# Two orders changed in a three-layer kernel: chunk 2's place in a pair, and drains before weight stages

## Chip, cores and metric

The kernel runs on one core of a Trainium2 chip. The metric is the device time of one execution in microseconds (us), taken as the median of several runs. The profile is of one execution of its own.

## What is computed

The reference chains three layers over 1536 tokens of width 512. First comes attention with 8 heads over two sequences of 768, with a window and a few sink positions. Then a two-layer block with 2048 hidden units:

```python
h = x @ w_in
g = np.maximum(h, 0.0) + alpha * np.minimum(h, 0.0)
return (g @ w_out).astype(np.float32)
```

Last come four experts of 1024 hidden units, weighted per token:

```python
for e in range(E):
    h = np.maximum(x @ w1[e], 0.0)
    out += p[:, e:e + 1] * (h @ w2[e])
```

All inputs are 32-bit floats. The kernel splits each matrix operand into a rounded high part and a low part (hi, lo) and adds three products, hi·hi, hi·lo and lo·hi, so a logical matmul is three on TensorE (PE).

## The kernel before, in words

**Tiling.** Tokens are cut into three chunks (c = 0, 1, 2) of 512 columns, or six units of 256. Hidden units are cut into 48 slices of 128 (NW): 16 of the second layer (N1), then 32 of the experts. A slice k has a weight tile pair wh[k], wl[k] that holds both its first-layer and its second-layer weights. `s1` (lines 250 to 252) makes a slice's hidden values h for one chunk with 12 matmuls; `s2_transposed` (259 to 261) and `s2_natural` (268 to 270) add the slice into the output sums in PSUM, again 12 matmuls. Between them stands `prelu` (283 to 286: two operations on VectorE (DVE), one on ScalarE (ACT) for the high part gh, one on GpSimd (POOL) for the low part gl) or `relu` (292 on ACT, 297 on DVE).

**Weight stages.** Raw weights come by DMA from the SP queue into four buffers. `half(j)` (lines 102 to 122) turns half a slice into hi and lo parts in three stages that use ACT (102, 104, 120), DVE (107 to 109, sometimes 122) and POOL (110, sometimes 122). `pair(j)` (135, 136, 143) does so for two expert slices in eight stages, on ACT and POOL alone. `tick()` starts the next generator in a queue and moves every generator in flight by one stage; `ready(k)` ticks until slice k is complete. So where a tick stands in the program sets where the stage's instructions stand in the in-order queues of ACT, DVE and POOL. A load is issued by `load_due` once the buffer's last reader has been written out.

**fast and rest.** `fast` runs the attention, mixed with the second layer's slices 0 to 5 for units 0 to 4, in a loop over p whose last turn is p = NP + 3. `rest` runs the remaining steps in a list: unit 5 with slices 0 to 5 (256 columns), then three blocks of slices (6 to 10, 11 to 15, and the first two of the experts, 16 and 17) for each of the three chunks. In turn i it writes out `s1` and `prelu` or `relu` of step i and `s2` of step i - 2, then one tick, and, at the last slice of a block, four drains of the PSUM sums into the accumulators acc (lines 859, 862 or 871 on DVE; at block 2 also lines 864 and 865, the split of the new x). `sums` (313 to 326) makes combinations of the accumulators that the experts need, seven pieces in all, one per turn.

**Experts.** From slice 18 (PAIR1) on, slices go in pairs, 15 of them. For the first layer of chunks 0 and 1 together `four(k)` (lines 354 to 366) computes seven block products, 42 matmuls, in place of eight. Its last two low parts, of c21 and c12, are put into `self.later` as functions that `leave` runs. `out(k, c, hid)` (395 to 400) is the second layer of a pair for one chunk: four output tiles d of six matmuls each, every one followed by one DVE operation that adds the weighted result to acc (line 400). Its PSUM tiles alternate between two buffers, so tile d + 2 waits for the acc of tile d. `out` runs one waiting function of `later` after each acc, and ticks after d = 1 and d = 3. Chunk 2 has a plain first layer: `s1` for both slices.

In `experts` a turn is: four(k); out of chunk 2 of the pair before, whose hidden values were kept in `last`; s1 and relu of chunk 2 for this pair; one tick; what is left in `later`; out of chunks 0 and 1. After the last turn chunk 2's out of the last pair follows, and at that pair each acc is followed by its output DMA.

Of the kernel before, what the change touches and what calls it, by code (L numbers as in the profile page):

```python
# [28 lines left out]
N1 = F1 // P  # L29
NW = N1 + E * (F2 // P)  # L30
# [15 lines left out]
STARTS = [1, 3, 5, 9, 10, 12, 13, 14, 16, 18, 20, 22, 46, 48, 49, 50]  # L46
# [7 lines left out]
class Body:  # L54
# [70 lines left out]
    def pair(self, j):  # L125
# [16 lines left out]
        def minus(out, a, b):  # L142
            nc.gpsimd.tensor_tensor(out, a, b, ALU.subtract)
# [191 lines left out]
    def four(self, k):  # L335
# [26 lines left out]
        def add(out, a, b):  # L362
            nc.vector.tensor_tensor(out, a, b, ALU.add)  # L363
# [23 lines left out]
    def out(self, k, c, hid):  # L387

        nc, mm, e = self.nc, self.nc.tensor.matmul, (k - N1) * P // F2
        for d in range(CH // P):  # L390
            ps = self.psum[1].tile([P, CH], F32, tag="o", name=f"o{k}_{c}_{d}", bufs=2)
            n = slice(d * P, (d + 1) * P)
            for x, (hh, hl) in enumerate(hid):
                wh, wl = self.wh[k + x][:, CH:], self.wl[k + x][:, CH:]
                mm(ps, hh[:, n], wh, start=x == 0, stop=False)  # L395
                mm(ps, hh[:, n], wl, start=False, stop=False)  # L396
                mm(ps, hl[:, n], wh, start=False, stop=x == 1)  # L397
            nt = c * (CH // P) + d
            acc = self.acc[c][:, d, :]
            nc.vector.scalar_tensor_tensor(acc, ps, self.prob[:, nt, e:e + 1], acc, ALU.mult, ALU.add)  # L400
            self.leave(1)
            if d % 2:
                self.load_due()
                self.tick()
            if k == NW - 2:
                nc.sync.dma_start(self.a["out"][nt * P:(nt + 1) * P, :], acc)

    def leave(self, n=None):
        for step in self.later[:n]:
            step()  # L410
        del self.later[:n]

    def experts(self):
        last = None
        for k in range(PAIR1, NW, 2):
            if k > PAIR1:
                self.four(k)
            if last:
                self.out(k - 2, 2, last)
            if k + 4 < NW:  # L420
                self.queue.append(2 * (k + 4))
            last = []
            for x in range(2):
                ps = self.psum[0].tile([P, CH], F32, tag="o", name=f"h{k}_c{x}", bufs=2)
                self.s1(k + x, self.xh[2], self.xl[2], ps)
                last.append(self.relu(ps, f"{k}_c{x}"))
            self.load_due()
            self.tick()
            self.leave()
            for c in range(2):  # L430
                self.out(k, c, self.hid[k][c])
        self.out(NW - 2, 2, last)


    def positions(self):
# [251 lines left out]
    def fast(self):  # L687
# [5 lines left out]
        with tc.tile_pool(name="psa", bufs=1, space=PSUM) as self.psa:  # L693
# [10 lines left out]
            NP, items, before = NU * H, [], None  # L704
# [10 lines left out]
            for p in range(NP + 4):  # L715
                if p + 1 >= WHOLE:
                    self.at_load(p + QK + 1)
                self.at_split(p + 2)
                for j in [0, 1] if p == 0 else [p + 1] if p + 1 < SOON else [] if p < SOON else [p]:
                    self.at_scores(j)  # L720
                    if j == 0:
                        self.busy(psb, BETWEEN, "busy", tag="h", bufs=2)
                    if j < WHOLE:
                        self.at_load(j + QK)
                if p > max(LOADS) or p in LOADS:
                    self.load_due(1)
                if FILL.get(p):
                    self.busy(psb, FILL[p], f"busy{p}", tag="h", bufs=2)
                self.at_mask(p)
                if p == 1:  # L730
                    next(self.later_masks)
                if p % 2:
                    self.at_sinks(p - 3)
                self.at_exp(p)
                if p % 2 == 0:
                    self.at_values(p - 4)
                    self.at_scale(p - 4)
                    self.at_norm(p - 2)
                self.at_split_lo(p + 2)
                if p == 2 * H:  # L740
                    self.shares()
                turn = [p - 1]
                while items and items[0][0] < p + 1:
                    _, what, step = items.pop(0)
                    u, f, first, last = step
                    n = slice(u % 2 * UN, (u % 2 + 1) * UN)
                    if what == "s1":
                        ps = psb.tile([P, CH], F32, tag="h", name=f"h{u}_{f}", bufs=2)
                        self.ready(f)
                        self.s1(f, self.xh[u // 2][:, :, n], self.xl[u // 2][:, :, n], ps[:, :UN])  # L750
                        while turn:
                            self.at_turn(turn.pop())
                        gs[step] = self.prelu(tmp, ps[:, :UN], UN, f, f"a{u}_{f}")
                        continue
                    if first:
                        outs = [psb.tile([P, 2, UN], F32, tag="o", name=f"o{u}_{f}_{i}", bufs=2) for i in range(2)]
                    self.s2_transposed(
                        f, *gs.pop(step), [outs[d // 2][:, d % 2, :] for d in range(4)], first, last, [True, False] * 2
                    )
                    while turn:  # L760
                        self.at_turn(turn.pop())
                    if last:
                        for i in range(2):
                            acc = self.acc[u // 2][:, 2 * i:2 * i + 2, n]
                            if u in seen:
                                nc.vector.tensor_tensor(acc, outs[i], acc, ALU.add)
                            else:
                                nc.vector.tensor_copy(acc, outs[i])
                        seen.add(u)
                while turn:  # L770
                    self.at_turn(turn.pop())
                if p % 2 == 0:
                    self.at_x(p - 4)
                if p == NP + 3:
                    tmp.release()
                    at.release()
                    self.add_late()
                self.tick(p in STARTS)
                if p == NP - 1:
                    self.atk.release()  # L780
                    self.add_late()
                    self.plan(*range(EARLY, SLOTS))
# [12 lines left out]
    def rest(self, pool, units, blk0):  # L795

        nc, tc = self.nc, self.tc
        n1 = len(BLOCKS) - 1
# [4 lines left out]
        last = {s[3]: i for i, s in enumerate(steps)}  # L803
# [5 lines left out]
        sums = self.sums()  # L809
        with tc.tile_pool(name="psc", bufs=1, space=PSUM) as psc:  # L810
            psum = self.psum = [self.psb, psc]
            gs, outs = {}, None
            for i in range(len(steps) + 2):
                if i < len(steps):
                    k, c, n, f = steps[i]
# [10 lines left out]
                self.leave()  # L826
                i -= 2
                if i < 0:
                    continue
                k, c, n, f = steps[i]  # L830
                nn = n.stop - n.start
                f0, f1 = BLOCKS[k][0], BLOCKS[k][0] + BLOCKS[k][1] - 1
# [13 lines left out]
                while PAIR1 <= nxt < PAIR1 + 4 and last[nxt + 1 - SLOTS] <= i:  # L846
                    self.queue.append(2 * nxt)
                    nxt += 2
                self.tick()
                if (k, c) in [(n1 - 1, 2), (n1, 0), (n1, 1)] and (c, f) != (1, N1 + 1):  # L850
                    next(sums, None)
                if f < f1:
                    continue
                if k == n1 - 1:
                    self.new_x(c, "y")
                for d in range(4):
                    acc = self.acc[c][:, d, n]
                    if k == 0:
                        nc.vector.tensor_copy(acc, outs[d])
                        continue  # L860
                    if k < n1:
                        nc.vector.tensor_tensor(acc, outs[d], acc, ALU.add)
                        if k == n1 - 1:
                            nc.scalar.activation(self.xh[c][:, d, :], acc, AF.Copy)
                            nc.gpsimd.tensor_tensor(
                                self.xl[c][:, d, :], acc, self.xh[c][:, d, :].bitcast(F32), ALU.subtract
                            )
                        continue
                    nt = c * (CH // P) + d
                    pr = self.prob[:, nt, k - n1:k - n1 + 1]  # L870
                    nc.vector.tensor_scalar(acc, outs[d], pr, None, ALU.mult)
            self.experts()


# [147 lines left out]
```

## Time and profile before

| what | us |
|---|---|
| median of 3 runs | 923.92 |
| lowest and highest run | 923.84, 926.82 |
| the profiled execution's own time | 927.69 |
| its span from the first to the last instruction | 925.5 |

Times in the profile count from the span's start. In that execution `rest` begins on PE at about 212 us, the first pair of experts at 431 us, and the second pair at 463 us. A pair from the second on takes 32.3 us. PE, DVE, ACT and POOL each work through their queue in order; a bracket behind a row gives the idle time of the engine before the instruction and what ended it.

### The profile page before, as it was taken

How to read it: one execution, taken by the hardware profiler on the slowest of the kernel's cores; microseconds unless marked ns; L12 is line 12 of the kernel's file. 1: busy time of each engine (PE TensorE's matmuls, PEld its weight loads, DVE VectorE, ACT ScalarE, POOL GpSimd, SP SyncE). 2: the span in 40 equal slices, each digit the busy share in tenths (PEclk: the TensorE clock that was granted, in tenths of full speed). 3: DMA queues.
4: the chain of work that ended last, by engine and by line, in shares of the span. 5: the costliest groups of instructions: out<-in, count | busy, mean ns of one | idle time of the engine just before them, and what ended most of it. 6: DMA issues, size and time to landing. Idle time of an engine off the chain costs nothing.

```text
span 925.5 us, 12401 instructions
## 1 busy us (share of the span) xinstructions
PE 903.0 (98%) x4670; PEld 742.2 (80%) x4670; DVE 549.3 (59%) x999; ACT 316.2 (34%) x719; POOL 371.6 (40%) x346
## 2 busy tenths in 40 slices
PE   8999999998999999999999999999999999999997
PEld 5678999998878888887878777877887787778786
DVE  6578877647994553546555455455545545554554
ACT  4587767754331222332222121222212122221210
POOL 2366654535673454674414332341433234143100
PEclk9699999999999999999999999999999999999999
DMA  6554442201331010011011101110110101010003
GB/s 187 153 166 146 157 127 91 76 1 69 134 118 46 23 68 1 1 35 35 23 47 35 46 11 46 35 37 20 35 46 12 46 34 42 16 37 9 1 1 141
DMA packets 23718, 54.47 MB, mean 59 GB/s; under 512 B 3168, under 2 KB 3168, under 8 KB 23648
## 3 DMA queue, kind: packets, MB, share of 16 engines
q1 hardware_dynamic: 23504, 53.57, 17.6%
q8 instruction: 39, 0.64, 0.3%
q14 instruction: 31, 0.25, 0.1%
q10 hardware_dynamic: 144, 0.00, 0.0%
HBM read 50.42 MB, written 3.15 MB: 58 GB/s over the span
## 4 chain that ended last, share of the span: by engine, by line
PE 85%; DVE 12%; issue 1%; ACT 1%; POOL 0%; DVEq 0%; ACTq 0%; POOLq 0%
PE o L395 8%; PE o L397 8%; PE o L396 8%; PE h L354 5%; PE h L356 5%; PE h L355 5%; PE h L250 4%; PE h L251 4%; PE h L252 4%; PE o L259 4%; PE o L260 4%; PE o L261 4%; PE pv L646 3%; PE h_c L250 3%; PE h_c L251 3%; PE h_c L252 3%
## 5 line engine op out<-in xcount | busy, mean ns | idle before, releaser
L136 POOL TENSOR_TENSOR wl<-wraw,wh 128x512 fp32r<-128x512 f32 x60 | 78.3, 1306 | 294.0 <-ACT wh L135 294.0
L400 DVE SCALAR_TENSOR_TENSOR acc<-o,prob,acc 128x512 f32<-128x512 f32 x180 | 134.8, 749 | 77.4 <-PE o L397 76.5
L395 PE MATMUL o<-wh,hh 128*128 128x512 f32 x240 | 93.4, 389 | 0.0
L396 PE MATMUL o<-wl,hh 128*128 128x512 f32 x240 | 93.4, 389 | 0.0
L397 PE MATMUL o<-wh,hl 128*128 128x512 f32 x240 | 93.4, 389 | 0.0
L250 PE MATMUL h<-xh,wh 128*128 128x256 f32 (+1 forms) x264 | 90.4, 342 | 0.0
L252 PE MATMUL h<-xh,wl 128*128 128x256 f32 (+1 forms) x264 | 87.9, 333 | 0.0
L251 PE MATMUL h<-xl,wh 128*128 128x256 f32 (+1 forms) x264 | 87.8, 332 | 0.0
L286 POOL TENSOR_TENSOR gl<-qk,gh 128x512 fp32r<-128x512 f32 (+1 forms) x36 | 49.2, 1369 | 77.8 <-ACT gh L285 75.5
L285 ACT ACTIVATE gh<-qk 128x512 fp32r<-128x512 f32 (+1 forms) x36 | 21.5, 598 | 123.4 <-DVE qk L284 123.4
L297 DVE SCALAR_TENSOR_TENSOR hl_c<-h_c,hh_c 128x512 fp32r<-128x512 f32 x30 | 20.8, 693 | 71.1 <-ACT hh_c L292 71.1
L292 ACT ACTIVATE hh_c<-h_c 128x512 fp32r<-128x512 f32 x30 | 18.0, 599 | 131.7 <-PE h_c L252 131.7
L363 DVE TENSOR_TENSOR wraw<-h,wraw 128x512 f32<-128x512 f32 x45 | 31.1, 692 | 51.0 <-PE h L356 49.4
L283 DVE TENSOR_SCALAR qk<-h,alpha 128x512 f32<-128x512 f32 (+1 forms) x36 | 25.3, 703 | 57.3 <-PE h L252 56.7
L259 PE MATMUL o<-gh,wh 128*128 128x512 f32 (+1 forms) x144 | 54.4, 378 | 4.3 <-ACT gh L285 2.5
L366 ACT ACTIVATE wraw<-h 128x512 f32<-128x512 f32 x15 | 9.0, 599 | 137.9 <-PE h L356 137.9
L250 PEld LDWEIGHTS h<-xh,wh 128*128 128x128 f32 x264 | 50.1, 190 | 6.6 <-issue 1.7
L260 PE MATMUL o<-gl,wh 128*128 128x512 f32 (+1 forms) x144 | 54.5, 378 | 0.5 <-POOL gl L286 0.5
L395 PE MATMUL o<-wh,hh_c 128*128 128x512 f32 x120 | 48.3, 402 | 6.2 <-DVE acc L400 6.2
L261 PE MATMUL o<-gh,wl 128*128 128x512 f32 (+1 forms) x144 | 54.3, 377 | 0.0
L252 PEld LDWEIGHTS h<-xh,wl 128*128 128x128 f32 x264 | 50.0, 189 | 5.3 <-DVE wl L122 0.3
L251 PEld LDWEIGHTS h<-xl,wh 128*128 128x128 f32 x264 | 50.1, 190 | 4.9
(172 smaller groups left out, 2388.8 us busy)
## 6 DMA issues: line engine op xcount, KB each, us to landing
wraw<-in_w SPq DMA_DIRECT2D x32, 512.0 KB, 3.6
wraw<-in_w SPq DMA_DIRECT2D x64, 256.0 KB, 2.6
qk<-in_qk SPq DMA_DIRECT2D x21, 352.0 KB, 2.9
v<-in_v SPq DMA_DIRECT2D x12, 256.0 KB, 3.2
out<-acc SPq DMA_DIRECT2D x12, 256.0 KB, 2.2
qk<-in_qk SPq DMA_DIRECT2D x8, 272.0 KB, 3.3
qk<-in_qk SPq DMA_DIRECT2D x11, 176.0 KB, 3.1
qk<-in_qk SPq DMA_DIRECT2D x8, 136.0 KB, 3.5
```

Source lines behind the costliest of these rows:

```text
L136: nc.gpsimd.tensor_tensor(lo, x, hi.bitcast(F32), ALU.subtract)
L250: mm(ps, wh[:, c], xh[:, dk, :], start=dk == 0, stop=False)
L251: mm(ps, wh[:, c], xl[:, dk, :], start=False, stop=False)
L252: mm(ps, wl[:, c], xh[:, dk, :], start=False, stop=dk == DM // P - 1)
L259: mm(outs[dt], wh[:, c], gh, start=first and begins[dt], stop=False, skip_group_check=True)
L260: mm(outs[dt], wh[:, c], gl, start=False, stop=False, skip_group_check=True)
L261: mm(outs[dt], wl[:, c], gh, start=False, stop=last, skip_group_check=True)
L286: nc.gpsimd.tensor_tensor(gl, g, gh.bitcast(F32), ALU.subtract)
L395: mm(ps, hh[:, n], wh, start=x == 0, stop=False)
L396: mm(ps, hh[:, n], wl, start=False, stop=False)
L397: mm(ps, hl[:, n], wh, start=False, stop=x == 1)
L400: nc.vector.scalar_tensor_tensor(acc, ps, self.prob[:, nt, e:e + 1], acc, ALU.mult, ALU.add)
```

## The change

There are two parts.

**In the experts**, chunk 2's s1 stands directly behind four(k), and chunk 2's out of the same pair stands behind the outs of chunks 0 and 1. The waiting low parts of c21 and c12 are written out behind the first of the two s1 calls, ahead of chunk 2's own relu; `out` no longer runs them.

**In rest**, the drains of a block's sums stand ahead of the tick and of the piece of `sums`. The tick in the last turn of `fast` is dropped, and two ticks are added in the first two turns of `rest`, behind the prelu of steps 0 and 1. The list of turns that run `sums` is shortened to the seven that do something.

```diff
             nc.vector.scalar_tensor_tensor(acc, ps, self.prob[:, nt, e:e + 1], acc, ALU.mult, ALU.add)
-            self.leave(1)
             if d % 2:
...
-    def leave(self, n=None):
-        for step in self.later[:n]:
-            step()
-        del self.later[:n]
+    def leave(self):
+        while self.later:
+            self.later.pop(0)()
 
     def experts(self):
-        last = None
         for k in range(PAIR1, NW, 2):
             if k > PAIR1:
                 self.four(k)
-            if last:
-                self.out(k - 2, 2, last)
             if k + 4 < NW:
                 self.queue.append(2 * (k + 4))
             last = []
             for x in range(2):
                 ps = self.psum[0].tile([P, CH], F32, tag="o", name=f"h{k}_c{x}", bufs=2)
                 self.s1(k + x, self.xh[2], self.xl[2], ps)
+                self.leave()
                 last.append(self.relu(ps, f"{k}_c{x}"))
             self.load_due()
             self.tick()
-            self.leave()
-            for c in range(2):
-                self.out(k, c, self.hid[k][c])
-        self.out(NW - 2, 2, last)
+            for c, hid in enumerate(self.hid[k] + [last]):
+                self.out(k, c, hid)
...
-                self.tick(p in STARTS)
+                if p < NP + 3:
+                    self.tick(p in STARTS)
...
                 if i < 0:
+                    if units:
+                        self.tick()
                     continue
...
-                self.tick()
-                if (k, c) in [(n1 - 1, 2), (n1, 0), (n1, 1)] and (c, f) != (1, N1 + 1):
-                    next(sums, None)
-                if f < f1:
-                    continue
-                if k == n1 - 1:
+                if f == f1 and k == n1 - 1:
                     self.new_x(c, "y")
-                for d in range(4):
+                for d in range(4 if f == f1 else 0):
...
+                self.tick()
+                if (k, c) in [(n1 - 1, 2), (n1, 0)]:
+                    next(sums)
```

## Rows read from the trace of the kernel before

**Rows 1.** The page's part 1: busy us (share of the span), instructions, per engine.

```profile
PE 903.0 (98%) x4670; PEld 742.2 (80%) x4670; DVE 549.3 (59%) x999; ACT 316.2 (34%) x719; POOL 371.6 (40%) x346
```

**Rows 2.** Waits of PE: who waited for whom, total us, times, longest.

```profile
PE o L395 <- DVE acc L400: 6.2, 13, 0.5
PE o L259 <- ACT gh L285: 2.5, 1, 2.5
...
PE o L259 <- DVE acc L862: 1.8, 1, 1.8
...
PE o L268 <- DVE acc L871: 1.1, 1, 1.1
```

**Rows 3.** Timeline, third pair: start, us, engine, line, operation, [idle before].

```profile
505.08 0.39 PE L395 MATMUL o<-wh,hh_c 128*128 128x512 f32 x1
...
507.24 1.30 POOL L136 TENSOR_TENSOR wl<-wraw,wh 128x512 fp32r<-128x512 f32 x1 [12.10 <-ACT wh L135]
...
507.31 1.77 DVE L297 SCALAR_TENSOR_TENSOR hl<-qk,hh 128x512 fp32r<-128x512 f32 x1
...
509.01 0.74 DVE L400 SCALAR_TENSOR_TENSOR acc<-o,prob,acc 128x512 f32<-128x512 f32 x1
...
509.80 0.50 PE L395 MATMUL o<-wh,hh_c 128*128 128x512 f32 x1 [0.48 <-DVE acc L400]
...
511.31 0.39 PE L250 MATMUL h_c<-yh,wh 128*128 128x512 f32 x1
```

**Rows 4.** Timeline of DVE in the last pair.

```profile
895.05 0.68 DVE L297 SCALAR_TENSOR_TENSOR hl<-qk,hh 128x512 fp32r<-128x512 f32 x1
```

**Rows 5.** Timeline of PE in the last pair, the places of rows 3.

```profile
892.82 0.39 PE L395 MATMUL o<-wh,hh_c 128*128 128x512 f32 x1
...
898.26 0.39 PE L250 MATMUL h_c<-yh,wh 128*128 128x512 f32 x1
```

**Rows 6.** Timeline of POOL, one pair: first and last of eight.

```profile
550.55 1.30 POOL L136 TENSOR_TENSOR wl<-wraw,wh 128x512 fp32r<-128x512 f32 x1 [8.01 <-ACT wh L135]
...
557.22 1.30 POOL L136 TENSOR_TENSOR wl<-wraw,wh 128x512 fp32r<-128x512 f32 x1
```

**Rows 7.** Line 400: all 180 acc operations, ns min/median/max.

```profile
L400 DVE SCALAR_TENSOR_TENSOR acc<-o,prob,acc x180: 736/751/752, 453.7 to 920.2; 128x512 f32<-128x512 f32 x180
```

**Rows 8.** Timeline of PE where rest begins, steps 2, 0 and 1.

```profile
212.79 0.28 PE L250 MATMUL h<-xh,wh 128*128 128x256 f32 x1
...
216.99 0.28 PE L252 MATMUL h<-xh,wl 128*128 128x256 f32 x1
219.73 0.38 PE L259 MATMUL o<-gh,wh 128*128 128x256 f32 x1 [2.46 <-ACT gh L285]
220.59 0.58 PE L260 MATMUL o<-gl,wh 128*128 128x256 f32 x1 [0.48 <-POOL gl L286]
...
224.80 0.28 PE L259 MATMUL o<-gh,wh 128*128 128x256 f32 x1
```

**Rows 9.** Windows: length, busy us by engine, PE's granted clock, DMA.

```profile
220.00:224.00 4.00, 3.52 (x18) 3.41 (x18) 1.22 (x3) 2.51 (x5) 1.96 (x3) 0.57 0.31 100
```

**Rows 10.** Timeline of DVE, same place: end of fast, first prelu.

```profile
214.16 1.28 DVE L768 COPY acc<-o 128x512 f32<-128x512 f32 x2
...
218.17 0.48 DVE L283 TENSOR_SCALAR qk<-h,alpha 128x256 f32<-128x256 f32 x1
```

**Rows 11.** Timeline of DVE at the drain of slices 6 to 10, chunk 0.

```profile
270.54 1.65 DVE L109 SCALAR_TENSOR_TENSOR wraw<-cm,wraw 128x512 int32<-128x512 int32 x1
272.12 2.47 DVE L862 TENSOR_TENSOR acc<-o,acc 128x512 f32<-128x512 f32 x4
```

**Rows 12.** Timeline of DVE at sums, ahead of line 871's drain.

```profile
418.54 3.40 DVE L314 TENSOR_TENSOR yl<-wraw,yh 128x512 fp32r<-128x512 f32 x2 [0.87 <-ACT yh L313]
```

**Rows 13.** Waits of PE's weight loads (PEld), columns as in rows 2.

```profile
PEld h L252 <- DVE wl L122: 0.3, 1, 0.3
```

**Rows 14.** DMA issues, raw weights: count, KB each, us to landing.

```profile
wraw<-in_w SPq DMA_DIRECT2D x32, 512.0 KB, 3.6
```

## Prediction

> **What bounds the kernel now.** I read the page first. TensorE is busy 98% of the span, the next engine 59% [rows 1]; so time can come only from PE's own idle stretches, and the question is how many of these the two new orders close. The second view is therefore the list of PE's waits [rows 2]. One row stands out by its count: 13 times a second-layer matmul of line 395 waits for an accumulator operation of line 400. The other three come once each, all in the part called rest: a gh, and two drains of a block's sums.
>
> The third view is the timeline around one of the 13. In chunk 2's out the accumulator operation of tile d = 1 starts at 509.01, because DVE first ran a waiting low part (line 297) of 1.77 us, and PE's next tile starts only at 509.80 after an idle 0.48 [rows 3]. That low part took so long beside POOL, which began a weight piece at 507.24 [rows 3]; in the last pair, where no weights are left, the same operation takes 0.68 [rows 4] and nothing waits. What a wait costs is more than its idle figure, since PE also restarts slowly: chunk 2's out lasts from 505.08 to 511.31, 6.23 us [rows 3], against 892.82 to 898.26, 5.44 us, in the last pair [rows 5]. So one wait of 0.48 costs 0.79, that is 0.31 beyond its idle time.
>
> **The change, part by part.** No matmul, no DVE operation and no DMA is added or removed: the same instructions come in another order. *Experts.* The stall needs two things at once: low parts in DVE's queue between accumulator operations, and PSUM tiles that alternate between two buffers. The change takes the first away. Behind four(k) PE now runs chunk 2's s1, 24 matmuls, 5.4 us at the rate of the last pair [rows 5], and these wait for no DVE result of four(k). In that time DVE does the last addition of four (taken at 0.74, as the accumulator operation [rows 3]) and the two low parts: with 0.68 for each of these [rows 4] 2.1 us, and with 1.77 for each [rows 3] 4.3 us. Both fit under 5.4, so out of chunk 0, which needs c12's low part, finds it ready. Gain: 13 x 0.79 = 10.3 us.
>
> What is late next there? Every moved instruction has to be placed. The last two weight pieces of a pair (ticks in chunk 2's out) move from behind four(k + 2) to ahead of it. POOL then does its burst of eight, 550.55 to 558.52 [rows 6], and these two, some 3 us, in one run of 11 us, behind chunk 2's second relu. Three outs last 3 x 5.44 = 16.3 us [rows 5], so POOL is done before four begins, and DVE's waiting low parts meet no POOL. The burst does lie beside accumulator operations, but it did so before, and all 180 took 736 to 752 ns [rows 7]. ACT's pieces go in front of its first copy in four; they finish with POOL's burst. The SP queue's raw loads follow the pieces that free the buffers, so none is later against its use. The last pair's outs and the output DMAs keep their place at the end: nothing there.
>
> *Start of rest.* PE finishes the s1 of steps 0 to 2 at 216.99, waits until 219.73 for gh and until 220.59 for gl, and starts step 1's s2 at 224.80 [rows 8]. The wait also lowered the granted clock: 0.57 over 220 to 224 [rows 9], that is mostly the 1.2 GHz level instead of 2.4, behind 2.7 us without a matmul. Before it, 35 starts of matmuls of 256 columns took from 212.79 to 216.99 [rows 8], 0.12 us each, so the 25 starts from 216.99 to 224.80 need 3.0 of these 7.8 us: 4.8 us lost. The cause is DVE's order: the sums are copied by 215.44, but prelu starts at 218.17 [rows 10], because the stages of fast's last tick stand between. The change puts these 2.7 us of stages behind prelu of step 0. Prelu then starts at 215.44. From prelu's start to the second matmul took 220.59 - 218.17 = 2.42 us, so that matmul comes at 217.86, where a PE without waits would have it at 217.23: 0.63 still lost. Step 1's prelu comes behind 0.95 of prelu and 2.7 of stages, at 219.1, its second matmul at 221.5, wanted at 217.86 + 24 x 0.12 = 220.7: 0.8 still lost. Gain 4.8 - 1.4 = 3.4 us. Gaps so short should not lower the clock: in the pairs a wait of 0.48 costs 0.79 in all [rows 3, 5]. Upper end 4.8; lower end 1.4, if steps 1 and 2 each lose 1 us more because a single stage operation of line 109 takes 1.65, as at 270.54 [rows 11], where all the stages between copy and prelu took 2.7 here.
>
> On this term a rule bears: the Trainium skill, "SBUF — State Buffer", section "Who interferes with whom", says that a DVE instruction with two SBUF inputs is held by a GpSimd instruction that reads SBUF for all of that instruction's time, and a DVE instruction with one SBUF input is not. The slow row of line 297 and the steady rows of line 400 agree. The rule speaks against the new order here, since stages with two SBUF inputs now run beside POOL's gl; by it the lower end, and a sum of 15.2, would be right.
>
> *Drains in front.* PE waits 1.8 us for a drain that DVE reaches only at 272.12, behind a stage operation of 1.65 us that began at 270.54 and others before it [rows 2, 11]. The drain needs only matmuls that PE ended before a whole s1 (2.7 us), so at the head of the queue it is done in time: gain 1.8 + 0.3 = 2.1. The drain near 421.9 stands behind two pieces of sums of 3.40 us [rows 12]; moved ahead, it gains 1.1 + 0.3 = 1.4 [rows 2]. The stages and pieces now wait for 2.5 us of drain instead; their results are needed one turn (24 matmuls, 5.4 us) later or more. Bounds for these two: 2.5 (one of them half kept) to 3.9, with the small waits on drains elsewhere.
>
> **Sum.** 10.3 + 3.4 + 2.1 + 1.4 = 17.2 us. The profiled execution took 927.69, its span 925.5; so such an execution would take 910.5. It lies 3.8 above the median of 923.92; I take the gain as the same there: **906.7**. Bounds of the terms: 9.5 (one pair keeps its wait) to 10.3, 1.4 to 4.8, 2.5 to 3.9; with them 904.9 to 910.5.
>
> **Rivals.** (a) *The weights take it back.* The slices of the first block come just in time now: a weight load of line 252 once waits 0.3 us for a low part that DVE makes in line 122 [rows 13]. A PE that arrives 3.4 us earlier would wait there for as long, and the 2.1 of the drain behind it may go the same way. Against it: the two added ticks start the stages of slices 7 to 10 one turn earlier, and following the queue by hand, only one forced tick of ready(k) is left there instead of two. Time: 923.9 - 10.3 - 1.4 = 912.2.
>
> (b) *The 13 waits move instead of going.* If chunk 0's out found c12's low part late, or POOL's run reached into four, the 0.79 would be paid elsewhere in each pair. Against it is the slack of 1.1 to 3.3 us worked out above. Time: 923.9 - 6.9 = 917.0.
>
> (c) *Slower: ACT is held by a raw load.* A stage begins with an ACT operation on a raw buffer. Started one turn earlier, it may stand at the head of ACT's queue while the load, 3.6 us to landing [rows 14], is still under way, with the next gh behind it and PE behind that. It is only the place from step 0 to slice 13, 12 halves; it decides once more than 17.2 / 3.6, about five, of them hold PE for the whole landing. With all twelve it gives 906.7 + 43 = 950. Against it: loads are issued as early against the stages as before, two turns ahead.
>
> (d) *Nothing moves:* the 13 waits have another cause that the order leaves alone: 923.9. The undisturbed last pair speaks against it.
>
> **How the numbers follow.** Forecast 0.78, (a) 0.10, (b) 0.06, (c) 0.03, (d) 0.03. The range reaches from 903.5, a little under the forecast's own lower bound, for what runs differ, to 912.5, which takes in (a): together 0.88, less some for sizes outside the bounds. About 0.3% (2.8 us) is what a measurement of this kernel can tell from no change. The forecast, (a) and (b) are faster, (d) is the same, (c) slower: 0.94, 0.03, 0.03.
>
> **What would show it.** Right: the row of 13 waits of line 395 is gone, chunk 2's out takes 5.4 us in every pair, a pair from four to four 31.5 instead of 32.3, the low parts of line 297 from qk all take near 0.7, and line 400 stays at 0.75. At the start of rest no gap of PE over 1 us and a clock of 1.00 over 220 to 224; no wait for line 862, or for line 871 ahead of line 268. Wrong: a new wait of PE in s1 of slice 10 (a), on line 297 ahead of line 395 (b), or ACT waiting on raw weights between 215 and 280 (c).

## The result, and the profile after

| us | before | after |
|---|---|---|
| median | 923.88 (4 runs, 922.47 to 926.82) | 911.19 (4 runs, 906.78 to 911.72) |
| profiled execution, its span | 927.69, 925.5 | 906.78, 905.0 |

The ratio is 0.985, 95% interval 0.9817 to 0.9884, so the kernel is faster by 1.5%, clear of no change. The time lies within the range that was given (903.5 to 912.5), 4.5 us above its point of 906.7 and 0.7 above 910.5, up to which the bounds of the forecast's own terms reached. One program does not always take the same time here: how long PE's granted clock stays low near 22 us differs between executions, and since the profiled execution of after has a short fall and that of before a long one, the two spans may not simply be subtracted.

PE is still what bounds the kernel; DVE, which lost 19 us of busy time against [rows 1], ran no operation less. The page of after, part 1:

```profile
PE 891.7 (99%) x4670; PEld 739.1 (82%) x4670; DVE 530.0 (59%) x999; ACT 317.2 (35%) x719; POOL 365.0 (40%) x346
```

The waits of PE in after (who waits for whom, total us, times, longest):

```profile
PE o L260 <- POOL gl L286: 1.9, 3, 0.8
...
PE o L259 <- ACT gh L285: 0.5, 1, 0.5
```

All four rows of [rows 2] have gone or shrunk: the 13 waits and both drains are not there, the 2.5 for gh is 0.5. One wait has grown: before, PE waited once for the low part gl of line 286, for 0.48 [rows 8]; now it does so three times, for 1.9 in all.

Where the time went is seen by cutting the span at four of PE's matmuls: the first s1 of `rest`, the first s1 of 512 columns behind unit 5, the first matmul of the first `four`, and the last matmul of all. The first column below is the time of the first of these starts in the timeline, the next three are the times from each to the next, and behind the span stands the mean granted clock over 20 to 40 us.

| us | rest begins | unit 5 | blocks, to the first four | experts | span | clock |
|---|---|---|---|---|---|---|
| before | 212.79 | 19.21 | 199.04 | 488.76 | 925.5 | 0.57 |
| after | 207.84 | 17.86 | 195.20 | 478.31 | 905.0 | 0.91 |
| change | (−4.95) | −1.35 | −3.84 | −10.45 | | |
| experts_only | 212.19 | 19.18 | 198.73 | 478.29 | 914.2 | 0.57 |
| rest_only | 212.53 | 17.86 | 195.20 | 488.63 | 919.9 | 0.57 |
| drains_only | 207.79 | 20.36 | 196.24 | 488.59 | 918.7 | 0.91 |
| quiet_out2 | 207.80 | 19.15 | 198.72 | 478.27 | 909.9 | 0.91 |
| after_again | 207.86 | 17.72 | 195.20 | 478.31 | 905.0 | 0.91 |
| no_first_ticks | 207.84 | 14.99 | 197.73 | 478.28 | 904.9 | 0.91 |
| second_tick_only | 212.63 | 16.03 | 195.82 | 478.29 | 908.5 | 0.57 |
| more_fill | 207.31 | 17.84 | 195.20 | 478.27 | 904.4 | 1.00 |
| before_fill | 208.09 | 20.47 | 198.72 | 488.65 | 921.7 | 1.00 |
| fill_second_tick | 207.43 | 16.03 | 195.20 | 478.28 | 902.9 | 1.00 |
| leave_late | 207.91 | 17.84 | 195.20 | 553.81 | 980.7 | 1.00 |

In this pair of profiles the change is worth 1.35 + 3.84 + 10.45 = 15.6 us; the 4.95 ahead of `rest` is not its doing. Kernels without any edit of that stage show 212.2 to 212.8 with a clock of 0.57 in one execution and 207.8 with 0.91 in another: experts_only and quiet_out2 run the same program up to there. Two of the three terms depend on the pair that is taken. The five kernels that start `rest` as before does take 19.15 to 20.47 for unit 5, and the three others with the blocks as before take 198.72 or 198.73 for them, not 199.04. Between before_fill and more_fill the sum is 2.63 + 3.52 + 10.38 = 16.5 us.

In the experts the timeline of PE in the third pair of after shows chunk 2's out from 515.92 to the next four at 521.36:

```profile
515.92 0.39 PE L395 MATMUL o<-wh,hh_c 128*128 128x512 f32 x1
...
521.36 0.39 PE L354 MATMUL h<-yh,wh 128*128 128x512 f32 x1
```

That is 5.44 us instead of the 6.23 of [rows 3]. All low parts of line 297, and all acc operations of line 400, in after (ns, least/median/most):

```profile
L297 DVE SCALAR_TENSOR_TENSOR hl<-qk,hh x30: 680/687/694, 431.5 to 879.3; 128x512 fp32r<-128x512 f32 x30
...
L400 DVE SCALAR_TENSOR_TENSOR acc<-o,prob,acc x180: 750/751/752, 443.6 to 899.6; 128x512 f32<-128x512 f32 x180
```

No low part takes the 1.77 of [rows 3] any more, and line 400 stays where [rows 7] had it.

At the start of `rest` four short waits are left. PE in after:

```profile
212.77 0.39 PE L260 MATMUL o<-gl,wh 128*128 128x256 f32 x1 [0.34 <-POOL gl L286]
...
216.29 0.39 PE L259 MATMUL o<-gh,wh 128*128 128x256 f32 x1 [0.51 <-ACT gh L285]
...
217.49 0.39 PE L260 MATMUL o<-gl,wh 128*128 128x256 f32 x1 [0.81 <-POOL gl L286]
...
224.28 0.39 PE L260 MATMUL o<-gl,wh 128*128 128x256 f32 x1 [0.79 <-POOL gl L286]
```

They come at steps 0, 1 (two) and 3, together 2.45 us of idle time. The clock does not fall there: the windows of after (length, busy us of PE, PEld, DVE, ACT, POOL, granted clock, DMA share, GB/s) have 1.00 where [rows 9] had 0.57:

```profile
216.00:220.00 4.00, 2.89 (x22) 2.69 (x23) 2.77 (x5) 1.93 (x5) 3.20 (x3) 1.00 0.57 207
220.00:224.00 4.00, 3.50 (x30) 3.29 (x28) 2.90 (x6) 1.99 (x4) 0.99 (x2) 1.00 0.44 160
```

The reason for the waits is in DVE's queue. The weights of the second layer arrive as 64-bit floats (not every input has 32 bits, as was said at the start): half a slice, 128x512 values, is 512 KB [rows 14]. Lines 102 to 110 make a 32-bit float of the two words of each value; these are the stages that share DVE and POOL with prelu here. The timeline of DVE in after, from the prelu of step 0 (210.40) past those of steps 1 (214.86) and 3 (221.65):

```profile
210.40 0.48 DVE L283 TENSOR_SCALAR qk<-h,alpha 128x256 f32<-128x256 f32 x1
...
212.00 1.27 DVE L109 SCALAR_TENSOR_TENSOR wraw<-cm,wraw 128x512 int32<-128x512 int32 x1
213.63 1.31 DVE L122 TENSOR_TENSOR wl<-wraw,wh 128x512 fp32r<-128x512 f32 x1 [0.36 <-ACT wh L120]
214.86 0.47 DVE L283 TENSOR_SCALAR qk<-h,alpha 128x256 f32<-128x256 f32 x1
...
221.04 0.69 DVE L122 TENSOR_TENSOR wl<-wraw,wh 128x512 fp32r<-128x512 f32 x1 [2.19 <-ACT wh L120]
221.65 0.48 DVE L283 TENSOR_SCALAR qk<-h,alpha 128x256 f32<-128x256 f32 x1
```

and POOL over the first part of it:

```profile
211.99 0.73 POOL L286 TENSOR_TENSOR gl<-qk,gh 128x256 fp32r<-128x256 f32 x1 [0.31 <-ACT gh L285]
213.35 1.04 POOL L110 TENSOR_TENSOR wraw<-wraw 128x512 int32<-128x512 int32 x1 [0.63 <-DVE wraw L109]
```

Two stage operations that take 0.69 where POOL is quiet (as at 221.04) take 1.27 and 1.31 beside these two, each of which had started first. So the prelu of step 1 starts 4.46 us behind that of step 0, and the prelu of step 3 stands behind a stage for which DVE waits 2.19 us on ACT.

The drains now start DVE's work of their turn. DVE in after, at the two places of [rows 11, 12]:

```profile
260.69 2.47 DVE L854 TENSOR_TENSOR acc<-o,acc 128x512 f32<-128x512 f32 x4
263.08 1.28 DVE L107 TENSOR_SCALAR wraw<-wraw 128x512 int32<-128x512 uint32 x1
...
408.80 2.72 DVE L863 TENSOR_SCALAR acc<-o,prob 128x512 f32<-128x512 f32 x4
411.43 2.38 DVE L314 TENSOR_TENSOR yl<-wraw,yh 128x512 fp32r<-128x512 f32 x2
```

### The profile page after: what moved, and what is told of

Read it like the earlier page. It is cut to its first block, busy times and chain, and to the rows that moved or that the text cites. A ratio compares the mean times of both kernels' runs of the same rounds, so it can differ in the third digit from the quotient of the medians.

```text
span 905.0 us, 12418 instructions
## 1 busy us (share of the span) xinstructions
PE 891.7 (99%) x4670; PEld 739.1 (82%) x4670; DVE 530.0 (59%) x999; ACT 317.2 (35%) x719; POOL 365.0 (40%) x346
## 4 chain that ended last, share of the span: by engine, by line
PE 92%; DVE 4%; ACT 1%; issue 1%; POOL 0%; DVEq 0%; ACTq 0%; POOLq 0%
PE o L397 9%; PE o L396 9%; PE o L395 9%; PE h L354 5%; PE h L356 5%; PE h L355 5%; PE h L250 5%; PE h L251 5%; PE h L252 5%; PE o L259 5%; PE o L260 5%; PE o L261 4%; PE h_c L250 3%; PE pv L640 3%; PE h_c L251 3%; PE h_c L252 3%
## 5 line engine op out<-in xcount | busy, mean ns | idle before, releaser
L572 ACT ACTIVATE p<-p,nmax 128x288 f32<-128x288 f32 (+1 forms) x96 | 47.8, 500 | 15.9 <-DVE nmax L551 15.8
L396 PEld LDWEIGHTS o<-wl,hh 128*128 128x128 f32 x240 | 45.0, 188 | 9.4
L395 PEld LDWEIGHTS o<-wh,hh 128*128 128x128 f32 x240 | 45.0, 188 | 9.4
```

## The experiments

Line numbers shift by a few from kernel to kernel; the stages of the table above are meant throughout. Where nothing else is said, the ratio is to the kernel before in the same set of runs.

**The two halves of the change.** experts_only is the first part of the diff alone:

```diff
-            if last:
-                self.out(k - 2, 2, last)
...
+                self.leave()
                 last.append(self.relu(ps, f"{k}_c{x}"))
...
+            for c, hid in enumerate(self.hid[k] + [last]):
+                self.out(k, c, hid)
```

> The changed order of the experts with rest as before. Theory (the two parts are independent, 13 waits at 0.79 us each): the 13 waits of line 395 for line 400 go, the pairs become 31.5 us long, the waits at the start of rest and on the two drains stay as in rows 2; 10.3 us less than before. Rival (the parts lean on each other: part of the gain in the pairs came from rest reaching them in another state): some of the 13 waits stay, gain under 8 us.

Measured 916.33 (912.92 to 918.06, 6 runs), ratio 0.9895 [0.986, 0.9929]. PE's waits:

```profile
PE o L259 <- ACT gh L285: 2.5, 1, 2.5
...
PE o L259 <- DVE acc L856: 1.8, 1, 1.8
...
PE o L268 <- DVE acc L865: 1.1, 1, 1.1
```

As expected, the 13 are gone, the three of `rest` are all there, and the experts take the 478.3 of after. rest_only is the second part alone:

```diff
-                self.tick(p in STARTS)
+                if p < NP + 3:
+                    self.tick(p in STARTS)
...
+                    if units:
+                        self.tick()
...
+                self.tick()
+                if (k, c) in [(n1 - 1, 2), (n1, 0)]:
+                    next(sums)
             self.experts()
```

> The changed order of rest with the experts as before. Theory: the 13 waits stay at 0.48 each; the experts start 5.2 us earlier after the start of rest than before (1.3 us at unit 5's steps, 3.9 us at the drains); 5 us less than before. Rival (the earlier arrival is given back in the experts): under 2.8 us less.

Measured 921.26 (915.48 to 922.09, 12 runs), ratio 0.994 [0.9916, 0.9964]. PE's waits:

```profile
PE o L395 <- DVE acc L400: 6.2, 13, 0.5
PE o L260 <- POOL gl L286: 1.9, 3, 0.8
```

Here the 13 stay and the three waits for gl appear. Stage by stage the halves add up to the change, with no interplay: −10.45 in the experts from one, −1.35 and −3.84 from the other.

**The drains without the ticks.** drains_only is the kernel before with the drains ahead of tick and sums, and with the last tick of `fast` left where it was:

```diff
-                self.tick()
...
-                if k == n1 - 1:
+                if f == f1 and k == n1 - 1:
                     self.new_x(c, "y")
-                for d in range(4):
+                for d in range(4 if f == f1 else 0):
...
+                self.tick()
```

> Only the drains ahead of the tick and of sums; the ticks at the start of rest and the experts as before. Theory: the waits on line 862 and on line 871 ahead of line 268 go, the wait of 2.5 us for gh at the start stays with its stretch at half clock; 3.5 to 3.9 us less than before. Rival (the drains are in time only because the two early ticks moved the weight stages ahead): a wait for a weight part or a drain near slice 10 of 1 us or more remains; 1.4 to 2.5 us less.

Measured 919.97 (917.93 to 924.76, 12 runs), ratio 0.9961 [0.9934, 0.9987]. The blocks take 196.24, that is 2.8 less than in before and 2.5 less than in the other kernels with the old blocks, under the 3.5 to 3.9 of the theory and over what its rival left. Waits of PE:

```profile
PE o L259 <- ACT gh L285: 2.5, 1, 2.5
...
PE h L252 <- POOL wl L122: 0.3, 1, 0.3
```

Both waits on drains are gone, and the wait for gh stays as expected. New is an s1, of slice 9, that waits for its weights. So the drains in front give most of the blocks' gain, but about 1 us of it (196.24 against 195.20) is kept only if the stages start earlier, as the two added ticks make them.

**Is it POOL beside the low parts?** quiet_out2 leaves the old order of the experts and takes only the weight pieces away from chunk 2's out: its two ticks go behind the out of chunk 1.

```diff
-            if d % 2:
+            if d % 2 and c < 2:
                 self.load_due()
                 self.tick()
...
             for c in range(2):
                 self.out(k, c, self.hid[k][c])
+            for _ in range(2):
+                self.load_due()
+                self.tick()
```

> The order of before in the experts and in rest, but the two ticks inside chunk 2's out are moved behind chunk 1's out, so that POOL has no weight piece while DVE runs the two waiting low parts. Theory (the wait comes from low parts that POOL stretches to 1.77 and 1.10 us): every low part from qk takes 0.68 to 0.70, the 13 waits go without the new place of chunk 2's first layer, and the time falls by 10.3 us, as with the new order. Rival (two more DVE operations in the queue between the accumulations are enough, with or without POOL): the 13 waits stay, shorter or not, and the time falls by under 3 us.

Measured 910.67 (909.03 to 917.18, 6 runs), ratio 0.9859 [0.9817, 0.9902]. The low parts, between the same acc operations as before:

```profile
L297 DVE SCALAR_TENSOR_TENSOR hl<-qk,hh x30: 679/682/693, 436.2 to 880.6; 128x512 fp32r<-128x512 f32 x30
```

The experts take 478.27, as with the new order. The ticks carry copies on ACT as well, but in after 15 of the 30 low parts ran beside an operation of ACT and took 0.68. So the cause of the 13 waits was not the low parts' place by itself but the place beside POOL's weight pieces. Either cure does: move the low parts, or move the pieces.

**The same kernel again.** after_again is the changed kernel without an edit, to see how its executions spread.

> The changed kernel once more, to have its runs beside the others on one chip. Both theories: executions fall into groups by the granted clock of the core, as before's do (919.3 at 0.999, 922.3 at 0.995, 926.8 at 0.988). Theory (the groups come from the clock in the first 60 us, which the change does not touch): the same groups lie 15 to 16 us lower, some 911.3 at 0.989 and 904 to 907 above. Rival (the new order makes the core's clock fall less): the groups are not parallel, and 0.988 is missing.

Measured 905.2 (904.94 to 906.76, 6 runs), ratio 0.9781 [0.9752, 0.981]. All six have a mean granted clock of 0.998 or 0.999, as the profiled execution has with 0.997; the other three of the four executions behind the 911.19 had 0.989 (911.05 to 911.72). The kernel before shows 919.2 to 919.8 at 0.999, 922.0 to 923.9 at 0.994 or 0.995, and 926.1 to 929.9 at 0.986 to 0.991. Like against like, 926.8 less 911.3 is 15.5, as the theory has it, but at 0.999 the middle of each, 919.5 less 905.1, is 14.4, less than it said.

**The price of the added ticks.** no_first_ticks drops them:

```diff
-                    if units:
-                        self.tick()
                     continue
```

> The changed kernel without the two ticks in the first two turns of rest (the last tick of the attention loop stays dropped). Theory (the waits that are left at the start of rest, 3.3 us, come from the stages of these ticks between the first prelus): the steps of unit 5 take 14.5 to 15.5 us instead of 17.9, but slices 9 and 10 are staged one turn later and PE waits there for 1 to 3 us, as the rival on the weights in the prediction said; within 1.5 us of the changed kernel. Rival (the staging has slack): no wait at slices 9 and 10, 2.5 to 3.3 us faster.

Measured 910.87 (904.8 to 911.97, 6 runs), ratio 0.9831 [0.9796, 0.9867]. Unit 5 falls from 17.86 to 14.99, but the blocks rise from 195.20 to 197.73. Both are as the theory has them. PE's waits and the place of the first:

```profile
PE h L252 <- POOL wl L122: 1.8, 1, 1.8
...
PE o L260 <- POOL gl L286: 0.3, 1, 0.3
...
239.26 0.50 PE L252 MATMUL h<-xh,wl 128*128 128x512 f32 x1 [1.81 <-POOL wl L122]
```

This is rival (a) of the prediction at work, in s1 of slice 9: a PE that arrives 2.9 us earlier meets weights that are not ready, and 2.5 of the 2.9 are paid there. So the two added ticks gain nothing over none: 14.99 + 197.73 = 212.72 us without them, 213.06 with them. They only carry the loss from one place to another. second_tick_only keeps one of the two:

```diff
-                    if units:
+                    if units and i == -1:
                         self.tick()
```

> The changed kernel with a tick in the second turn of rest only. Following the queue by hand, the stages are as far along from turn 3 on as with both ticks. Theory (the place of the stages between the prelus sets what is lost): the waits before step 1's second layer, 1.7 us, go, one of up to 1 us before step 2's or step 3's stays; 1 to 2 us faster than the changed kernel. Rival (the chain from ACT to DVE to POOL is what limits, wherever the ticks stand): the waits only move by a step; within 0.6 us of the changed kernel.

Measured 909.72 (908.85 to 910.41, 6 runs), ratio 0.9827 [0.9798, 0.9855], all six at a mean clock of 0.989 to 0.991. From the start of `rest` to the first four it takes 16.03 + 195.82 = 211.85, against 213.06 in after. PE's waits:

```profile
PE o L260 <- POOL gl L286: 1.1, 2, 0.8
...
PE h L252 <- DVE wl L122: 0.2, 1, 0.2
```

One tick is enough for the weights but for 0.2 us, and costs less at the start. Over this stretch it beats after by 1.2 us, as the theory had it; against the executions of after at 0.989 it is 1.6 us faster.

**The clock ahead of rest.** more_fill is the changed kernel with two more filler matmuls in turn 3 of `fast` and one more in turn 4 (a filler reads no result and keeps PE at work); before_fill is the same edit in the kernel before.

```diff
-WARM, FILL = 6, {p: 1 for p in range(11)}
+WARM, FILL = 6, {p: {3: 3, 4: 2}.get(p, 1) for p in range(11)}
```

> The changed kernel with two more filling matmuls in turn 3 of the attention loop and one more in turn 4, where PE stands idle for 0.6 and 1.0 us at about 20 us and the granted clock then falls for 4 to 15 us. They compute nothing that is used. Theory (these idle stretches let the clock fall): the clock stays at 1.00 over 20 to 40 us in the profile, the group of executions at 0.988 is gone, and the median falls by 4 to 7 us. Rival (the clock falls whatever stands there): the same groups, each 0 to 1.5 us later for the added matmuls.

> The kernel before with the same three added filling matmuls. Theory (the clock's fall at 20 us is one and the same in both kernels and the fill removes it): one group of executions at a clock of 0.998 or more, 919 to 921 us; so against the changed kernel with the fill (905.9 to 906.5) the change is worth 13 to 15 us when the clock does not interfere. Rival (the fill works in the changed kernel alone): groups at 922 and 927 remain.

more_fill measured 906.3 (905.87 to 906.54, 6 runs), ratio 0.979 [0.9762, 0.9819]; before_fill 922.54 (920.31 to 925.78, 12 runs), ratio 0.997 [0.9945, 0.9995]. Windows of before, of after and of more_fill, one fence each:

```profile
20.00:40.00 20.00, 18.52 (x60) 10.98 (x61) 10.98 (x41) 8.04 (x27) 6.25 (x7) 0.57 0.57 181
```
```profile
20.00:40.00 20.00, 17.91 (x91) 10.68 (x90) 14.62 (x52) 12.68 (x39) 6.94 (x8) 0.91 0.69 204
```
```profile
20.00:40.00 20.00, 17.43 (x98) 10.80 (x97) 15.90 (x55) 13.01 (x40) 7.96 (x9) 1.00 0.74 205
```

In the same 20 us the kernel before gets 60 recorded matmuls through and more_fill 98. With the fill no execution takes 911 us: more_fill's six lie within 0.7 us. Its median is 4.9 under the 911.19 but 1.1 over the 905.2 of after_again, so the fill buys steadiness, not speed over a good execution. For before_fill the theory failed: it expected one group at 919 to 921 us, but the twelve spread over 5.5 us at clocks of 0.993 to 0.999. Its profile has another fall, behind the wait for gh at the start of `rest`. Window of before_fill:

```profile
216.00:220.00 4.00, 4.00 (x19) 4.00 (x20) 1.48 (x3) 2.11 (x4) 1.26 (x2) 0.50 0.16 62
```

Unit 5 takes 20.47 there and 17.84 in more_fill, whose clock is 1.00 over the same 4 us: the change removes this fall with the wait. Between the two medians lie 16.2 us, more than the 13 to 15 expected.

**Both improvements.** fill_second_tick is after with the fill and the single tick (the two diffs above).

> The changed kernel with the fill and with a tick in the second turn of rest only. Theory (both gains add): 1.1 us less from the start of rest to the first four than the changed kernel has, all executions within 1 us of each other, 904.8 to 905.5. Rival (the gain of the single tick was the clock's doing in a run with a long fall): 906 to 906.5.

Measured 904.95 (904.78 to 906.0, 6 runs), ratio 0.9772 [0.9741, 0.9802]. That is 1.35 under more_fill, and all but the one at 906.0 lie where the theory put them; from the 905.2 of after_again it cannot be told apart. `rest` up to the first four takes 16.03 + 195.20 = 211.23, 1.8 less than after, and the row of weights that second_tick_only had is gone:

```profile
PE o L260 <- POOL gl L286: 1.1, 2, 0.8
...
PE h_c L250 <- DVE acc L863: 0.2, 1, 0.2
```

**Does the low parts' place matter, or chunk 2's alone?** leave_late is more_fill with the two low parts written out behind both s1 and relu of chunk 2, still ahead of the outs:

```diff
                 self.s1(k + x, self.xh[2], self.xl[2], ps)
-                self.leave()
                 last.append(self.relu(ps, f"{k}_c{x}"))
+            self.leave()
             self.load_due()
             self.tick()
```

> The changed kernel with the fill, and with the two waiting low parts written out behind both relus of chunk 2, where the kernel before had its last call, while chunk 2's first layer stays in its new place. Theory (the low parts of c21 and c12 must be done in the 5.4 us of chunk 2's first layer, ahead of POOL's run): DVE now gets to them only behind the second relu, 6.9 us after four, when POOL begins its run; they take 1.77 and 1.10 us again, and out of chunk 0 waits some 2 to 3.5 us for c12's low part in every pair: 30 to 50 us slower than with the fill alone, slower than before. Rival (the new place of chunk 2's first layer is what counts, wherever the low parts stand): no wait over 0.5 us, within 3 us of the changed kernel.

Measured 983.09 (982.07 to 984.67, 4 runs), ratio 1.0616 [1.0572, 1.066]: 76.8 over more_fill, far over the 30 to 50 expected. The waits of PE, all low parts of line 297, and the third pair on DVE, POOL and PE, in leave_late:

```profile
PE o L397 <- DVE hl L297: 48.5, 14, 3.7
...
L297 DVE SCALAR_TENSOR_TENSOR hl<-qk,hh x30: 680/1747/1771, 431.5 to 958.9; 128x512 fp32r<-128x512 f32 x30
```
```profile
513.14 1.27 POOL L136 TENSOR_TENSOR wl<-wraw,wh 128x512 fp32r<-128x512 f32 x1 [25.63 <-ACT wh L135]
513.18 3.44 DVE L297 SCALAR_TENSOR_TENSOR hl<-qk,hh 128x512 fp32r<-128x512 f32 x2
...
516.68 0.50 PE L397 MATMUL o<-wh,hl 128*128 128x512 f32 x1 [3.70 <-DVE hl L297]
```

Two low parts that took 0.68 each now take 3.44 together, started 0.04 us behind POOL's first piece, and PE stands 3.70 us in each of 12 pairs, less in the last two. In the last pair POOL has no piece, and the place alone is left:

```profile
958.33 1.28 DVE L297 SCALAR_TENSOR_TENSOR hl<-qk,hh 128x512 fp32r<-128x512 f32 x2
...
959.67 0.50 PE L397 MATMUL o<-wh,hl 128*128 128x512 f32 x1 [1.54 <-DVE hl L297]
```

So of each 3.70 the place behind the second relu is 1.54 and POOL 2.16. The waits are 48.5 of the 75.5 us that the experts lose against more_fill, about what was expected; the expectation left out what follows them. One pair, from 496.50 to 532.02, keeps a clock of 1.00 and takes 35.52, that is 31.51 + 3.70 + 0.31, with the 0.31 beyond the idle time that the prediction found. The other pairs with such a wait take 37.1 to 38.1, at a lower clock, as this window of leave_late shows (more_fill has 1.00 over the same 200 us):

```profile
600.00:800.00 200.00, 181.51 (x747) 146.50 (x746) 98.76 (x124) 38.16 (x66) 55.88 (x50) 0.94 0.08 27
```

So the new order is right by one place only: with chunk 2's first layer where it now is, the low parts must be done before POOL starts, and their place between the two s1 sees to that.

## Why the prediction was right or wrong

**Pairs: right.** 10.3 was forecast, 10.45 measured. The mechanism (low part stretched beside POOL, acc late, two buffers) is shown by quiet_out2, which moves the weight pieces alone, and from the other side by leave_late. Chunk 2's out of 5.44 and a pair of 31.50 (four at 489.86 and 521.36) are as written. Rivals (b) and (d) fall with it. Yet leave_late makes the condition of (b) come true, a late low part of c12, by one place in the program, and then the experts take 75.5 us more, some seven times the 10.3 that (b) put on it.

**Start of rest: right in kind, wrong in size.** The failed step is "Gain 4.8 - 1.4 = 3.4 us": 1.35 was measured, the lower end (2.63 between before_fill and more_fill). The sum left 1.4 us lost; 4.8 - 1.35 = 3.45 stayed lost, 2.45 of it idle time. Prelu of step 0 came where it was put, and the clock stayed at 1.00, as forecast. But the stages behind it were taken at the 2.7 us that they had cost ahead of it, as if a duration moved along with its operation. Of those 2.7, 1.57 are one operation of line 108 that started 0.03 us behind a piece of POOL:

```profile
215.32 1.32 POOL L122 TENSOR_TENSOR wl<-wraw,wh 128x512 fp32r<-128x512 f32 x1
...
215.35 1.57 DVE L108 TENSOR_SCALAR wraw<-wraw 128x512 int32<-128x512 int32 x1
```

In the new place line 108 takes 0.71, but lines 109 and 122 take 1.27 and 1.31 beside gl and a stage of POOL, and DVE stands 0.36 for ACT: from the end of that prelu to the next (211.25 to 214.86) it is 3.6. Step 3, which the sum gave no loss, lost 0.79 to a ping-pong of DVE and ACT: DVE waits 2.19 for a wh that ACT makes only behind the gh of step 2. The same 2.17 stood in DVE's queue before, under cover of a PE that was late anyway. The prediction looked for cover of what moved, not for what lost its cover when PE came sooner.

The Trainium skill, "SBUF — State Buffer", section "Who interferes with whom", as the prediction applied it, put the sum at 15.2. The 15.6 measured is near it, in part by luck: the lower end was reached by way of step 3 as well, on which neither sum had put a loss. The trace agrees where DVE has two SBUF inputs: lines 109, 122 and the low parts of line 297 were stretched, and line 400 with one stayed at 750 to 752 ns. But line 108 has one SBUF input and was stretched too, from 0.42 (at 215.71 in after) to 1.57. The section says that one input does not contend only outside what it calls the 2-port perf modes, a condition that the prediction left out; whether line 108 ran in such a mode no row here shows.

**Drains: right.** 3.5 forecast, 3.84 measured, 3.52 against the other kernels with the old blocks. That the stages behind them were due only a turn later held with the added ticks (no wait for weights in the blocks of after) and failed without them: 1 us in drains_only, 2.5 in no_first_ticks. Rival (a) is therefore real, and what keeps it off is the added ticks, for which the prediction argued in one sentence and to which it gave no price; second_tick_only shows that one of the two does all but 0.2 us of it. With both, unit 5 takes 2.87 us more than in no_first_ticks, so the pair pays at the start what it saves in the blocks. (c) did not show: at this place ACT waits once for a raw load in after, 0.36 us at 248.38, where before had 2.31 and 0.38, and PE has no wait in the blocks.

**From one execution to the median: wrong.** The step "I take the gain as the same there" subtracted the gain from a median of 923.92. "Such an execution" was to take 910.5; the ones of after with the long fall take 911.05 to 911.72, 0.4 to 1.0 under the 912.1 that 927.69 less 15.6 gives. But the median of a few runs goes by how long the clock was low in most of them: 923.92 had a mean clock of 0.994, between the ends, three of the four executions of after had the long fall, and all of after_again had the short one, with 905.2. So of the 4.5 us by which the point missed, 1.6 are the terms and the other 2.9 are the clock of the executions on each side. It was luck that 911.19 fell inside the range: the terms reached only to 910.5, and the room above was left for rival (a), which did not come.

## What to carry to other kernels

In front of an in-order queue, write what PE waits for ahead of what is only due later, and look for every moved operation at which engine runs beside it in the new place, and which of the two starts first, since its duration is not its own. Ask also which stalls were covered by the wait that is taken away: here an idle 2.2 us of DVE came into sight. Before a gain is taken from a median, look at the granted clock of each execution, and compare like with like.

## What the runs showed of the hardware

- Near 22 us PE's granted clock falls to the 1.2 GHz level: in before it is 0.50 over 24 to 36 us, behind two idle stretches of 0.62 and 1.00 us. Timeline of PE in before, [idle before]:

```profile
20.43 0.41 PE L620 MATMUL pst<-ident,rw 128*128 128x128 f32 x2 [0.62 <-DVE rw L589]
...
22.41 1.65 PE L539 MATMUL s<-qk 64*128 64x128 f32 x4 [1.00 <-DVE nmax L557]
```

  The same program gets 0.57 over 20 to 40 us in one execution and 0.91 in another. after has idle stretches of 0.15 and 1.00 there and falls too (0.68 over 24 to 28 us); more_fill still has an idle 1.01 us at 22.52 and does not fall. So the idle time alone does not tell. What decides on the length of the fall within one program stays open; in the four profiles with the fillers ahead of it there is none.
- How much longer a DVE operation gets beside POOL goes by which starts first. The first low part of [rows 3] started when POOL's piece had 1.23 us left and took 1.09 more than its 0.68; the second, at 509.67, had 0.55 of the next piece left and took 0.42 more. In after, line 109 at 216.16 started 0.16 us ahead of gl and kept its 0.69, while gl took 1.12 instead of 0.73. So in these rows the one that starts second pays, and here it is DVE by what POOL has left, less some 0.13 us:

```profile
508.50 1.72 POOL L136 TENSOR_TENSOR tl<-t,th 128x512 fp32r<-128x512 f32 x1
...
509.67 1.10 DVE L297 SCALAR_TENSOR_TENSOR hl<-qk,hh 128x512 fp32r<-128x512 f32 x1
```

  No count of instructions shows it; DVE's busy time does, with 549.3 in [rows 1] and 530.0 after at the same 999 instructions.
